# Sliding-window attention and soft MoE in one program: 64 queries x 8 heads in a group, and values on 64x64 tiles

## The chip, the cores and the metric

The kernel runs on one core of a Trainium2 chip. The metric is the time of one execution in microseconds, the median of three runs. The engines are named as the profile names them: PE (TensorE, matmuls; PEld is its weight load), ACT (ScalarE), DVE (VectorE), POOL (GpSimd) and SP (SyncE), from which nearly all DMAs are issued. PE writes to PSUM only; the other engines carry results from there to SBUF.

## The reference: what is computed

There are B=8 batches, H=8 heads, S=576 positions and D=64 features per head; everything is f32.

```
scores = (q @ k.T) / 8 - slope[h] * |i - j|      # only where 0 <= i - j < 128, else -1e9
attn   = softmax(scores);  x = attn @ v          # x: 4608 tokens x 512 features
logits = x @ phi                                 # phi: 512 x 32 slots (8 experts x 4)
d = softmax over tokens (axis 0) of logits;  slot_input = d.T @ x
slot_out[e] = relu(slot_input[e] @ w1[e]) @ w2[e]        # 512 -> 1024 -> 512
c = softmax over slots (axis 1) of logits;   out = c @ slot_out
```

A query sees itself and the 127 positions before it. The weights w1 and w2 are 33.5 MB, q, k, v and the output 9.4 MB each.

## The kernel before

*Tiles and groups.* The tokens are cut into 36 tiles of 128 queries, `(b, t)`. t=0..3 are the four full blocks of a batch; t=4 (in odd batches) holds the 64 last queries of the batch before and of this one. A tile is worked in two groups, g=0 and 1, of 4 heads each: 72 groups of 128 queries x 4 heads. A group's four heads lie in PSUM as `s4[:, u]`, u = 0..3, one bank pair (`s4s`) for even groups and one for odd ones.

*Scores.* `scores` writes for each strip of 32 queries only the 160 keys in its window: bf16 matmuls with `ramp` lay down the distance penalty (L236), then q by k is added (L247), eight small tiles of 64 rows x 32 columns of the array side by side. So in columns 0 to 127 stand the keys of the block before, in 128 to 255 those of the block itself, and each query uses exactly 128 of them. `merge` puts these together in one place with a predicated copy of 4 x 128 columns (`copy_predicated`, L262 for t=1..3, L264 for t=4, L260 for t=0), `rowmax` and `bias` make the negative scaled maximum `nb`, and `expo` takes four exponentials of 128x128 on ACT, each with a row sum (`accum_out`, the ACTIVATION_READ_ACCUMULATOR in the trace).

*Values.* Two groups later `flip` transposes the four 128x128 blocks on PE into bank "pt", `split` copies them to SBUF on ACT and separates them on POOL into the part of the block itself (`pa`) and of the block before (`pp`), zeros elsewhere. Three groups later `values` multiplies both by v (L362; L367 for t=4) into bank "xp": per head and block a 128x128 weight load and 64 moving columns. `x_store` scales by the inverse row sums (`total` on POOL, `inverse` on DVE) and puts x into SBUF, `x_flip` and `x_keep` transpose it for the logits.

*The token work* comes once for four tiles: `logits`, a running maximum over tokens (`token_max`), exponentials, two transposes, `slot_sum` (d.T @ x) and `slot_add`; and the softmax over slots (`slots_max`, `slots_exp`, `slots_norm`) into `ln`.

*The end.* The last tiles drain, the lanes of the running maximum are joined, `slot_inputs` makes the experts' inputs; then come `hidden` (L734), `expert_out` (L770) and `combine` (L791) with the stores, in the order that `TAIL_ORDER` spells out; `turn` transposes parts of `ln` for `combine`.

*What sets the order.* Inside `manual_schedule` each engine runs its instructions in the order in which the code issues them, and SP its DMAs. One iteration of the main loop issues the softmax front of group i, the flip of i-2, the values of i-3 and the scores of i+1; `do(when, i, ...)` hangs the token work onto later iterations. Banks are single: whoever wants to write "pt", "xp", "xq" or "mi" waits until the reader of the last contents is done. The weights come in units of 512 KB: 36 into a ring (`wpool`) during the attention, 15 into SBUF that the attention has freed (`place`), 13 more into ring slots that `hidden` has freed.

Of the kernel before, what the change touches and what calls it, by code (L numbers as in the profile page):

```python
# [24 lines left out]
P = 128  # L25
NT = 5
# [26 lines left out]
TAIL_ORDER = '''s0 b0v b1a b2v e1n e13 k0 e12 c00 e15 c01 e16 s1 c02 e2n e24 k1 e22 c10 e25 c11 e25 s2 c12 e3n e34 k2 e32 c20 e35 c21 e35 s3 c22 k3 c30 c31 c32'''  # L53
# [11 lines left out]
def tile_attn_softmoe(  # L65
# [4 lines left out]
    vd: bass.AP,  # L70
    phid: bass.AP,
    w1d: bass.AP,
    w2d: bass.AP,
    slopes: bass.AP,
# [11 lines left out]
    mask_u = cst[:, 0:P].bitcast(I32)  # L86
    mask_t = cst[:, P:P + TAIL].bitcast(I32)
    delta = cst[:, P + TAIL:]
    pick, sel = cst[:, 0:P], cst[:, P:P + 2 * NS]
# [11 lines left out]
    kq = cpool.tile([P, 3 * UW], F32, name="kq")  # L101
    ramp = cpool.tile([P, 2, 2, WIN], BF16, name="ramp")
    ones = cpool.tile([P, P], BF16, name="ones")
    kt = cpool.tile([P, 6 * P], F32, name="kt")
    area = cpool.tile([P, 24, HW], F32, name="area")
# [3 lines left out]
    qs = [kq[:, NB * P + 2 * P * i:NB * P + 2 * P * i + 2 * P] for i in range(3)]  # L109
# [5 lines left out]
    vs = [area[:, i] for i in (7, 0, 1, 5)]  # L115
    v3_even, v4_even, v4_odd = area[:, 2], area[:, 3], area[:, 4]
    p4s = [quarters(area[:, i]) for i in (8, 9, 6)]
    pps = [quarters(area[:, i]) for i in (10, 11)]
    pas = [quarters(area[:, i]) for i in (12, 13)]
    xns = [area[:, i] for i in range(14, 14 + NXN)]  # L120
    xts = [quarters(area[:, i]) for i in range(20, 24)]
# [3 lines left out]
    areas = {i: area[:, i:i + 2].rearrange("p a w -> p (a w)") for i in range(0, 24, 2)}  # L125
    place = [ks[1], ks[0], ks[2]] + [areas[i] for i in (0, 14, 2, 4, 10, 8, 12, 6, 20, 22, 16, 18)]
# [20 lines left out]
    groups = [(b, t, g) for b, t in tiles for g in range(2)]  # L147
    number = {key: i for i, key in enumerate(groups)}
    n = len(groups)
# [8 lines left out]
    def load_q(i, eng=None):  # L158
        p, o = i // 18, 2 * P * (i % 18)
        (eng or nc.sync).dma_start(qs[i % 3], qd[p, :, o:o + 2 * P])  # L160
# [8 lines left out]
    v_slot = {}  # L169

    def load_v():
        if len(v_taken) < len(v_loads):
            b, t = v_loads[len(v_taken)]
            v_slot[b, t] = vs[len(v_taken) % 4]
            v_taken.append((b, t))
            nc.sync.dma_start(v_slot[b, t], vd[b, P * t:P * t + P])

    def load_v_tails(b):
        nc.sync.dma_start(v3_even, vd[b, 3 * P:4 * P])
        nc.sync.dma_start(v4_even[0:TAIL], vd[b, 4 * P:S])  # L180
        nc.sync.dma_start(v4_odd[0:TAIL], vd[b + 1, 4 * P:S])

    v_taken = []

    with tc.manual_schedule(engines=ORDERED):
        warm = area[:, 8].bitcast(BF16)[:, 0:512]
        nc.vector.memset(warm, 0.0)
        nc.vector.memset(low, LOW)
        nc.vector.memset(ramp, 0.0)
        nc.vector.memset(ones, 1.0)  # L190
        nc.gpsimd.memset(cst[:, 0:P], 1.0)
        nc.gpsimd.affine_select(cst[:, 0:P], cst[:, 0:P], [[1, P]], ALU.is_gt, 0.0, base=0, channel_multiplier=-1)
        load_k(0, 0)
        load_q(0, nc.scalar)
        for par in range(2):
            nc.sync.dma_start(ramp[64 * par:64 * par + 1], slopes[par:par + 1])
        load_q(1, nc.scalar)
        load_q(2, nc.scalar)
# [5 lines left out]
        nc.gpsimd.memset(area[:, 9, 0:P], 1.0)  # L204
# [5 lines left out]
        for t in range(2, 4):  # L210
            load_k(0, t)
# [343 lines left out]
    def loads(i):  # L555
# [3 lines left out]
        if i < 3:  # L559
            load_v()  # L560
# [362 lines left out]
```

## Time and profile before

| | |
|---|---|
| median of 3 runs | 322.65 us (322.46 to 322.69) |
| profiled execution | 324.43 us, its span 322.7 us |
| granted PE clock, mean | 0.96 |
| PE, DVE, ACT, POOL busy | 305.7, 181.8, 187.5, 85.3 us |
| DMA | 74.37 MB, mean 230 GB/s |
| first scores / last scores of the attention end | 5.85 / 245.96 us |
| first hidden-layer matmul | 264.15 us |

A line of the timeline gives start and duration in us, engine, source line, operation, what is written from what, and a count of instructions that were merged into it; in brackets the idle time ahead and who ended it. An f32 matmul shows as two records. A line of the groups has the busy time in us, the mean of one in ns and the idle time before it. A line of the windows gives start:end, its length, then the busy time of PE, PEld, DVE, ACT and POOL (with counts), the granted PE clock, the DMA engines' share and GB/s.

### The profile page before, as it was taken

Reading aid. Unit: us, or ns where it says so; the run is one execution under the profiler, and the core shown is the slowest. Engines: PE = TensorE matmul, PEld = TensorE weight load, DVE = VectorE, ACT = ScalarE, POOL = GpSimd, SP = SyncE. Lnnn points to the kernel's source line nnn. Section 1 sums busy time; section 2 is a strip of 40 time slices with the busy share of each in tenths; the row PEclk is TensorE's granted clock in tenths of the full one; section 3 lists DMA queues with packets and bytes.
Section 4 is the critical chain, followed back from the end, with each engine's and each line's share of the span. In section 5 each row is a group of like instructions: output and inputs, shape, how many; then the busy total and the mean of one; then the engine's idle time right before and its main releaser. Section 6 shows DMA issues by size and latency. Waiting matters only on the chain.

```text
span 322.7 us, 12515 instructions
## 1 busy us (share of the span) xinstructions
PE 305.7 (95%) x5143; PEld 241.8 (75%) x5143; DVE 181.8 (56%) x443; ACT 187.5 (58%) x769; POOL 85.3 (26%) x162
## 2 busy tenths in 40 slices
PE   7799999999999999999999999999999779999983
PEld 4589888988798799788979888888987623266641
DVE  3544666657675675776577567566746331124452
ACT  2746676677766866786767678766767310003342
POOL 2024413350431334234314342433434001000000
PEclk9659999999999999999999999999999975999998
DMA  7663345786686858687676786786524995995888
GB/s 204 219 182 112 105 148 165 219 282 212 206 307 199 264 175 261 201 281 238 204 240 203 235 257 216 232 258 189 174 72 130 359 387 163 331 399 199 333 346 314
DMA packets 35164, 74.37 MB, mean 230 GB/s; under 512 B 4226, under 2 KB 14116, under 8 KB 35108
## 3 DMA queue, kind: packets, MB, share of 16 engines
q1 hardware_dynamic: 34388, 73.07, 67.9%
q8 instruction: 40, 0.66, 0.8%
q10 hardware_dynamic: 720, 0.51, 0.5%
q14 instruction: 16, 0.13, 0.1%
HBM read 64.13 MB, written 9.44 MB: 228 GB/s over the span
## 4 chain that ended last, share of the span: by engine, by line
PE 88%; DVE 6%; issue 2%; ACT 1%; POOL 1%; DVEq 0%; ACTq 0%; POOLq 0%
PE xp L362 29%; PE pt L327 10%; PE s L247 9%; PE xq L382 6%; PE hp L734 6%; PE op L770 5%; PE s L236 4%; PE po L791 4%; PE ap L449 3%; PE lp L392 3%; PE xp L367 2%; PE s L229 2%; DVE area L373 1%; DVE s L282 1%; PE dp L414 1%
## 5 line engine op out<-in xcount | busy, mean ns | idle before, releaser
L317 ACT ACTIVATE area<-s,nb 128x128 f32<-128x128 f32 x288 | 102.5, 375 | 19.9 <-DVE nb L285 12.9
L362 PE MATMUL xp<-area 128*128 128x64 f32 x880 | 107.2, 275 | 0.0
L362 PEld LDWEIGHTS xp<-area 128*128 128x128 f32 x880 | 105.5, 195 | 0.0
L334 ACT COPY area<-pt 128x512 f32<-128x512 f32 x71 | 41.8, 588 | 56.8 <-PE pt L327 55.0
L317 ACT ACTIVATION_READ_ACCUMULATOR area<-s,nb 128x1 f32 x288 | 61.1, 212 | 0.0
L282 DVE TENSOR_REDUCE s<-s 128x4 f32<-128x512 f32 x71 | 49.6, 699 | 2.4
L336 POOL TENSOR_SCALAR_AFFINE_SELECT area<-area 128x512 f32<-128x512 f32 x48 | 30.6, 637 | 76.2 <-ACT area L334 75.9
L262 DVE COPY_PREDICATED s<-cst,s 128x512 f32<-128x512 int32 x48 | 33.2, 692 | 30.2 <-PE s L247 30.2
L327 PE MATMUL pt<-unit_r,area 128*128 128x128 f32 x284 | 46.0, 285 | 0.6 <-issue 0.4
L247 PE MATMUL s<-kq 64*32 64x160 f32 x1664 | 42.4, 306 | 0.0
L327 PEld LDWEIGHTS pt<-unit_r,area 128*128 128x128 f32 x284 | 32.9, 144 | 7.8 <-issue 5.2
L373 DVE TENSOR_TENSOR area<-xp,rs 128x512 f32<-128x512 f32 x35 | 24.1, 689 | 19.4 <-PE xp L362 16.2
L338 POOL TENSOR_SCALAR_AFFINE_SELECT area<-area 128x512 f32<-128x512 f32 x48 | 30.7, 639 | 3.3
L247 PEld LDWEIGHTS s<-kq 64*32 64x32 f32 x1664 | 29.7, 109 | 0.7
L289 POOL TENSOR_SCALAR rs<-sm 128x8 f32<-128x8 f32 x36 | 10.1, 280 | 74.0 <-ACT area L317 59.0
L382 PEld LDWEIGHTS xq<-unit_r,area 128*128 128x128 f32 x140 | 15.2, 143 | 14.2 <-DVE area L373 11.1
L382 PE MATMUL xq<-unit_r,area 128*128 128x128 f32 x140 | 23.1, 288 | 1.8 <-DVE area L373 1.4
L236 PE MATMUL s<-ramp,ones 64*32 64x320 bf16 x448 | 18.9, 314 | 2.0 <-ACT area L317 1.9
L385 ACT COPY area<-xq 128x512 f32<-128x512 f32 x35 | 20.4, 583 | 0.5 <-PE xq L382 0.5
L797 DVE COPY ob<-po 128x384 f32<-128x384 f32 x24 | 12.4, 553 | 12.4 <-PE po L791 12.4
L734 PE MATMUL hp<-w,inp 128*8 128x512 f32 (+1 forms) x128 | 18.6, 690 | 0.4 <-DVE inp L534 0.4
L260 DVE COPY_PREDICATED s<-cst,fine 128x512 f32<-128x512 int32 (+1 forms) x17 | 11.3, 664 | 11.9 <-PE s L229 7.6
(124 smaller groups left out, 288.0 us busy)
## 6 DMA issues: line engine op xcount, KB each, us to landing
w<-w SPq DMA_DIRECT2D x49, 512.0 KB, 5.1
area<-v_n SPq DMA_DIRECT2D x36, 256.0 KB, 3.6
out<-ob SPq DMA_DIRECT2D x24, 384.0 KB, 3.4
kq<-q_t SPq DMA_DIRECT2D x69, 128.0 KB, 3.1
kq<-k_t SPq DMA_DIRECT2D x32, 256.0 KB, 3.8
area<-w SPq DMA_DIRECT2D x12, 512.0 KB, 6.6
kt<-k_t SPq DMA_DIRECT2D x4, 384.0 KB, 3.8
kq<-w SPq DMA_DIRECT2D x3, 512.0 KB, 4.6
```

The costliest lines, as they stand in the source:

```text
L236: nc.tensor.matmul(s4[32 * c:32 * c + 32, 2 * par:2 * par + 2, 32 * r:32 * r + WIN], lhsT=ones[rows, 0:32], rhs=ramp[rows, g], start=True, ...
L247: nc.tensor.matmul(s4[32 * c:32 * c + 32, 2 * par + jj, 32 * r:32 * r + WIN], lhsT=qt[rows, jj, 32 * c:32 * c + 32], rhs=keys, start=False ...
L262: nc.vector.copy_predicated(s4[:, :, P:2 * P], bc(mask_u, 1, 4), s4[:, :, 0:P])
L282: nc.vector.tensor_reduce(st[key]["mx"][:, us], merged(key, us), axis=AX.X, op=ALU.max, negate=True)
L317: nc.scalar.activation(s["p4"][:, u], merged(key, u), AF.Exp, bias=s["nb"][:, u:u + 1], scale=SCALE, accum_out=st["sm", k][:, h:h + 1],)
L327: nc.tensor.transpose(s["pt"][:, u], s["p4"][:, u], ident)
L334: copy(pa[:, us], s["pt"][:, us])
L336: nc.gpsimd.affine_select(pp[:, us], pa[:, us], [[0, m], [-1, P]], ALU.is_gt, 0.0, base=0, channel_multiplier=1)
L338: nc.gpsimd.affine_select(pa[:, us], pa[:, us], [[0, m], [1, P]], ALU.is_ge, 0.0, base=0, channel_multiplier=-1)
L362: nc.tensor.matmul(xp[:, cols], lhsT=src, rhs=v_slot[b, t - 1 + ph][:, cols], start=(ph == 0 or t == 0), stop=(ph == 1))
L382: nc.tensor.transpose(st["xq", k][:, P * j:P * j + P], xns[k % NXN][:, P * j:P * j + P], ident)
L734: nc.tensor.matmul(hp[nb][NS * c:NS * c + w], lhsT=inp[:, o:o + w], rhs=wt[0, 4 * g + c, 2 * nb + kk][:, 512 * kp:512 * kp + 512], start=( ...
```

## The change

*Groups* become 64 queries x 8 heads: group g of a tile holds the strips g and g+2 of 32 queries. PSUM partitions are (head pair j, 32 queries), and `u` is (head parity, strip). The two groups of a tile are issued together, one iteration of the main loop is now a whole tile k: chains of k, flips of k-1, x_flip of k-3, `values` of k-2, scores of k+1, `values_off` of k-1.

*Merge.* Every query strip's window of 160 keys now starts at the same column, so only 32 columns have to be merged (`mask_le`, `mask_gt`), and exponentials read 128 columns from there. `t == 0` needs no other merge: the penalty ramp holds -1e30 where there are no keys.

*Row sums* come from a column of ones in v (66 columns per head, `VD`); exponentials have no `accum_out`, `total` and `inverse` go, and `x_store` adds EPS, takes the reciprocal and multiplies, per parity.

*Values.* Exponentials are written so that after the flip each 64x64 quarter is either full (it lies wholly inside the window) or triangular. `values_off` multiplies the full ones as soon as they are copied; `values` multiplies the triangular ones, once for the block before (`pps`) and once for the block itself, after `split` has cut them on POOL, in halves of 64 partitions and 256 elements. Both use 64x64 tiles of the array, four of them side by side. t=0 has no block before and uses 128x64.

*Banks* are "a", "b", "e", "o": the flips of the two groups go to "a" and "b", x_flip and slot_sum to "a" too, logits and the token flips to "b", the values to "e" and "o" by head parity. `x_keep` moves from ACT to DVE.

*Loads.* q comes in one DMA per tile (256 KB) into two buffers; the ring has 35 units, 15 go to freed places, 14 to freed ring slots; `sel` is loaded at the start. The penalty ramp and the masks come by DMA.

*The end.* `spin` issues bf16 matmuls of zeros between the steps of the drain; two of the three parts of `ln` are turned there already; `TAIL_ORDER` keeps the third.

The diff, cut to its core:

```diff
-TAIL_ORDER = '''s0 b0v b1a b2v e1n e13 k0 e12 ...
+TAIL_ORDER = '''s0 b2v e1n e13 k0 e12 ...
+VD = D + 2
...
+    def scores(k, g):
+        for par, rows in enumerate(half):
+            for j in range(NPAIR):
+                nc.tensor.matmul(
+                    parts[par][32 * j:32 * j + 32, :, 0:WIN], lhsT=slope[rows, j],
+                    rhs=steps[rows, 1 + 2 * g:3 + 2 * g] if t == 0 else bc(steps[rows, 0], 1, 2),
+                    start=True, stop=False)
+        for rr in range(2):
+            for par, rows in enumerate(half):
+                for j in range(NPAIR):
...
+                        r, o = g + 2 * rr, 0
+                        keys = kall[rows, 4 * (t - 1) + r:4 * (t - 1) + r + 5, j]
                     nc.tensor.matmul(
+                        parts[par][32 * j:32 * j + 32, rr, KB * o:WIN], lhsT=qt[rows, j, rr],
+                        rhs=keys, start=False, stop=(rr == 1))
...
+    def merge(k, g, us=ALL):
+        m = len(range(4)[us])
+        dst, src = (P, 0) if g else (0, P)
+        nc.vector.copy_predicated(
+            window(k, g, us, dst, KB), bc((mask_le, mask_gt)[g], 1, m), window(k, g, us, src, KB))
...
+            nc.scalar.activation(
+                dst, window(k, g, u, KB * g, P).rearrange("p (a w) -> p a w", a=2), AF.Exp,
+                bias=s["nb"][:, u:u + 1], scale=SCALE)
...
+    def take(k, g, copy):
+        copy(
+            pas[k % 2][:, :, :, KB * g:KB * g + KB],
+            st[k, g]["pt"].rearrange("p u (j w) -> p u j w", j=NPAIR))
+    def split(k, g):
+        for hf, rows in enumerate(half):
+            pa = pas[k % 2][rows, 2 * hf:2 * hf + 2, :, cols]
+            pp = pps[k % 2][rows, :, :, cols]
+            nc.gpsimd.affine_select(
+                pp, pa, [[0, 2 * NPAIR], [-1, KB]], ALU.is_gt, 0.0, base=-KB * g, channel_multiplier=1)
+            nc.gpsimd.affine_select(
+                pa, pa, [[0, 2 * NPAIR], [1, KB]], ALU.is_ge, 0.0, base=KB * g, channel_multiplier=-1)
...
+    def values_off(k, to=None):
+        for j in range(NPAIR):
+            for hf, par, rr in four(k):
+                nc.tensor.matmul(
+                    st["x", k][par][half[rr], j], lhsT=pas[k % 2][rows, places(k).index(2 * par + rr), j],
+                    rhs=v[rows, par, j], start=(j == 0), stop=False)
+    def values(k, to=None):
+        for j in range(NPAIR):
+            for kind in range(2):
+                for hf, par, rr in four(k):
+                    nc.tensor.matmul(
+                        st["x", k][par][half[rr], j], lhsT=pa[rows, at, j] if kind else pp[rows, at % 2, j],
+                        rhs=v[rows, par, j], start=False, stop=(j == NPAIR - 1 and kind == 1))
+    def x_store(k, pars=(0, 1)):
+        for par in pars:
+            nc.vector.tensor_scalar_add(rs[:, par], xp[par][:, :, D], EPS)
+        nc.vector.reciprocal(rs[:, pars[0]:pars[-1] + 1], rs[:, pars[0]:pars[-1] + 1])
+        for par in pars:
+            nc.vector.tensor_tensor(x[:, par], xp[par][:, :, 0:D], bc(rs[:, par], 2, D), op=ALU.mult)
...
+            chain(k, 1)
+            if k:
+                flip(k - 1, 0, "a")
+                flip(k - 1, 1, "b")
+                run("turn", k)
+            if k:
+                take(k - 1, 0, nc.scalar.copy)
+                split(k - 1, 0)
+                expo(k, 0)
+                take(k - 1, 1, nc.scalar.copy)
+                split(k - 1, 1)
+            run("keep", k)
+            expo(k, 1)
+            if k >= 2:
+                values(k - 2)
+            run("mid", k)
+            if k + 1 < n:
+                scores(k + 1, 0)
+                scores(k + 1, 1)
+                loads(k + 1)
+            if k >= 2:
+                after_values(k - 2)
+                x_store(k - 2)
+            if k:
+                values_off(k - 1)
...
+        spin(1)
+        turn(0, "a", free[1])
```

How the order on the engines moves, at three places. First PE in a steady tile. Before, on the way from one group's scores to the next (`xq` is x_flip, `pt` the flips, `xp` the values, `s_0` and `s_1` the scores' banks):

```order
L382 MATMUL xq<-unit_r,area 128x128 [waits DVE_49]
L382 MATMUL xq<-unit_r,area 128x128 x3
L327 MATMUL pt<-unit_r,area 128x128 [waits PE_49]
L327 MATMUL pt<-unit_r,area 128x128 x3
L362 MATMUL xp<-area 128x64 [waits DMAHW3_49,PE_49]
L362 MATMUL xp<-area 128x64 x3
L236 LDWEIGHTS ones
```

After, from the end of one tile's scores to the start of the next ones (L345 is `values_off`, L368 `values`, L305 the flips, L388 x_flip):

```order
L345 MATMUL xp<-va,area 64x66 [waits DVE_49,PE_49]
L345 MATMUL xp<-va,area 64x66 [waits DVE_49]
L345 MATMUL xp<-va,area 64x66 [waits DMAHW2_49]
L345 MATMUL xp<-va,area 64x66 x13
L305 MATMUL pt<-unit_r,area 128x128 x8
L388 MATMUL xq<-unit_r,xs 128x128 [waits Activation_49]
L388 MATMUL xq<-unit_r,xs 128x128 x3
L368 MATMUL xp<-va,area 64x66 [waits Pool_49] x2
L368 MATMUL xp<-va,area 64x66 x3
L368 MATMUL xp<-va,area 64x66 [waits Pool_49]
L368 MATMUL xp<-va,area 64x66 x26
```

The x_flip stood ahead of a group's flips and waited for DVE's x_store; now it stands behind the flips of both groups and waits for ACT, whose copy empties bank "a". `values_off` waits for DVE, which empties the banks "e" and "o".

Second, PE in a tile with the token flips (L439) and slot_sum (L451), after; before, the token flips (L414, L438) stood in two other groups and had a bank of their own ("mi"):

```order
L305 MATMUL pt<-unit_r,area 128x128 [waits Activation_49]
L305 MATMUL pt<-unit_r,area 128x128 x3
L439 MATMUL dp<-unit_r,lg 128x128 [waits Activation_49]
L439 MATMUL dp<-unit_r,lg 128x128
L388 MATMUL xq<-unit_r,xs 128x128 [waits DVE_49]
L388 MATMUL xq<-unit_r,xs 128x128
L388 MATMUL xq<-unit_r,xs 128x128 [waits DVE_49]
L388 MATMUL xq<-unit_r,xs 128x128
L356 MATMUL xp<-va,area 64x66 [waits DMAHW2_49]
L356 MATMUL xp<-va,area 64x66 x15
L451 MATMUL ap<-xs,dn 32x512 [waits DVE_49,Activation_49]
L451 MATMUL ap<-xs,dn 32x512 x3
```

The token flips now stand between the flips and x_flip, in bank "b", which the second flip has just filled and ACT must copy first; slot_sum waits for bank "a" and for the copied token flips.

Third, DVE. Before, for a tile without token work (L262 or L264 is the merge, L292 the inverse, L373 x_store):

```order
L264 COPY_PREDICATED s_0_84<-cst,s_0_84 128x4x64 [waits DMAHW7_49,PE_49,Activation_49]
L282 TENSOR_REDUCE s_0_84<-s_0_84 128x4 [waits DVE_49]
L285 TENSOR_SCALAR nb<-s_0_84 128x4 [waits DVE_49]
L373 TENSOR_TENSOR area<-xp,rs 128x512 [waits PE_49]
L264 COPY_PREDICATED s_1_85<-cst,s_1_85 128x4x64 [waits PE_49,Activation_49]
L282 TENSOR_REDUCE s_1_85<-s_1_85 128x4 [waits DVE_49]
L285 TENSOR_SCALAR nb<-s_1_85 128x4 [waits DVE_49]
```

After (L264 is the merge of 32 columns, L272 and L276 maximum and bias, L391 x_keep, L379 to L382 x_store):

```order
L264 COPY_PREDICATED s_0_86<-cst,s_0_86 128x4x32 [waits PE_49,Activation_49]
L272 TENSOR_REDUCE s_0_86<-s_0_86 128x4 [waits DVE_49]
L276 TENSOR_SCALAR nb<-s_0_86 128x4 [waits DVE_49]
L264 COPY_PREDICATED s_1_87<-cst,s_1_87 128x4x32 [waits PE_49,Activation_49]
L272 TENSOR_REDUCE s_1_87<-s_1_87 128x4 [waits DVE_49]
L276 TENSOR_SCALAR nb<-s_1_87 128x4 [waits DVE_49]
L391 COPY xs<-xq 128x512 [waits PE_49]
L379 TENSOR_SCALAR rs<-xp 128x4 [waits PE_49]
L379 TENSOR_SCALAR rs<-xp 128x4
L380 RECIPROCAL rs<-rs 128x8 [waits DVE_49]
L382 TENSOR_TENSOR xs<-xp,rs 128x256 [waits DVE_49]
L382 TENSOR_TENSOR xs<-xp,rs 128x256
```

x_keep has joined DVE and stands ahead of x_store, which has grown from one instruction to five; both chains of the tile stand ahead of them.

More of the change, by code (lines that the diff above doesn't have):

```diff
@@ L146, in tile_attn_softmoe @@
     tiles = [(b, t) for b in range(B) for t in order(b)]
-    groups = [(b, t, g) for b, t in tiles for g in range(2)]
-    number = {key: i for i, key in enumerate(groups)}
-    n = len(groups)
+    n = len(tiles)
     v_loads = [(b, t) for b in range(B) for t in range(4)]
@@ L322, in flip, with chain @@
[L322 to L335 removed]
+    def chain(k, g):
+        merge(k, g)
+        rowmax(k, g)
+        bias(k, g)
@@ L653, in tile_attn_softmoe, with spin @@
+            for _ in range(4):
+                filler()
+        ka, kb, kc = n - 3, n - 2, n - 1
+        lp = free[3]
+        idle = inp.bitcast(BF16)[:, 0:512]
+        def spin(m):
+            if "spin" not in st:
+                st["spin"] = bank("o", [P, 512], "spin")
+            for _ in range(m):
+                nc.tensor.matmul(st["spin"], lhsT=idle[:, 0:P], rhs=idle, start=True, stop=True)
         for _ in range(3):
             load_weight()
-        nc.sync.dma_start(pick[0:NS], seld[0:NS, 2 * NS:])
@@ L656, in tile_attn_softmoe @@
-        nc.sync.dma_start(sel, seld[:, 0:2 * NS])
-        x_store(ka)
-        inverse(kb)
+        nc.gpsimd.memset(inp, 0.0)
+        flip(kc, 0, "a")
+        flip(kc, 1, "b")
+        take(kc, 0, nc.scalar.copy)
+        take(kc, 1, nc.vector.tensor_copy)
+        x_flip(ka)
+        x_keep(ka)
+        values(kb)
+        for _ in range(5):
+            load_weight()
+        values(kc, [x.rearrange("p (j d) -> p j d", d=P)[:, :, 0:VD] for x in (free[0], free[2])])
+        x_store(kb)
+        run("act", n)
@@ L659, in tile_attn_softmoe @@
         run("dve", n)
+        x_store(kc, (0,))
+        x_store(kc, (1,))
         drain()
-        nc.gpsimd.memset(inp, 0.0)
-        flip(gc, to=quarters(free[0]))
-        load_weight()
-        split(gc, LO, nc.scalar.copy)
-        split(gc, HI, nc.vector.tensor_copy)
-        x_flip(ka)
-        values(gb, to=free[1])
-        x_keep(ka)
-        values(gc)
-        load_weight()
-        load_weight()
-        logits(final, range(3), to=lp)
-        x_store(kb, slice(0, 4))
-        x_store(kb, slice(4, 8))
@@ L675, in tile_attn_softmoe @@
-        x_flip(kb, free[2], range(0, 2))
-        x_flip(kb, js=range(2, 4))
-        x_keep(kb, nc.scalar.copy, slice(0, 2))
-        x_keep(kb, nc.vector.tensor_copy, slice(2, 4))
+        for _ in range(2):
+            load_weight()
+        spin(1)
+        turn(0, "a", free[1])
+        x_flip(kb, bank("b", [P, DM], "xq"))
+        x_keep(kb)
+        spin(1)
+        x_flip(kc, None, range(0, 2))
+        x_flip(kc, None, range(2, 4))
+        x_keep(kc, nc.scalar.copy, slice(0, 2))
+        x_keep(kc, nc.vector.tensor_copy, slice(2, 4))
```

567 lines of the change are left out of this document (253 added, 314 removed).

## The prediction

> **What bounds the kernel now.** I read the page's first and fourth parts, then the windows, then the timeline of one steady stretch.
>
> ```profile
> PE 305.7 (95%) x5143; PEld 241.8 (75%) x5143; DVE 181.8 (56%) x443; ACT 187.5 (58%) x769; POOL 85.3 (26%) x162
> PE 88%; DVE 6%; issue 2%; ACT 1%; POOL 1%; DVEq 0%; ACTq 0%; POOLq 0%
> 100.00:120.00 20.00, 19.99 (x370) 17.17 (x371) 13.44 (x33) 14.71 (x63) 5.68 (x11) 1.00 0.71 218
> ```
>
> TensorE (PE) carries 88% of the chain and is busy for 19.99 of 20 us in a steady window, with VectorE (DVE) at 13.4 and ScalarE (ACT) at 14.7. What it does there, for one group of 128 queries x 4 heads (two groups are a tile, 36 tiles in all):
>
> ```profile
> 109.23 0.42 PEld L382 LDWEIGHTS xq<-unit_r,area 128*128 128x128 f32 x4 [0.84 <-DVE area L373]
> 109.62 0.47 PEld L327 LDWEIGHTS pt<-unit_r,area 128*128 128x128 f32 x4
> 110.05 1.86 PEld L362 LDWEIGHTS xp<-area 128*128 128x128 f32 x16
> 110.42 0.59 ACT L334 COPY area<-pt 128x512 f32<-128x512 f32 x1 [0.48 <-PE pt L327]
> 111.99 0.33 PE L236 MATMUL s<-ramp,ones 64*32 64x320 bf16 x8
> 112.01 0.53 PEld L247 LDWEIGHTS s<-kq 64*32 64x32 f32 x32
> 112.79 0.42 PEld L327 LDWEIGHTS pt<-unit_r,area 128*128 128x128 f32 x4 [0.25 <-issue]
> ```
>
> From start to start: flips 0.43, values 1.94, scores 0.80, so 3.17 us a group without a hole. The values take most. Their 16 records (an f32 matmul is two records) need 0.116 us each, because each loads 128x128 weights for 64 moving columns. The scores put eight small tiles side by side: 32 records in 0.53, 16.6 ns each.
>
> **The change, part by part.** *Values.* Per tile of kind t=1..4 the 32 (t=4: 64) records become 96 on 64x64 tiles: 64 in `values`, 32 in `values_off`. No row shows 64x64. The nearest:
>
> ```profile
> 242.14 0.54 PEld L229 LDWEIGHTS s<-kq 64*128 64x128 f32 x8
> 247.91 1.01 PEld L367 LDWEIGHTS xp<-area 128*64 128x64 f32 x32 [0.17 <-issue]
> 235.13 0.81 PEld L392 LDWEIGHTS lp<-area,phi 128*32 128x32 f32 x32 [0.25 <-issue]
> 236.14 0.42 PEld L327 LDWEIGHTS pt<-unit_r,area 128*128 128x128 f32 x4 [0.20 <-issue]
> 261.04 1.07 PE L449 MATMUL ap<-area,dn 128*32 128x512 f32 x8
> ```
>
> Two column halves side by side give 31.6 ns a record (L367), two row halves 67 ns against 116 (L229). Both together lie between 31.6 (row halves gain nothing) and 15.8 (they gain fully); L229's 1.7-fold gain puts it at 18, the scores' eight tiles at 16.6. I take 17: `values` 1.09 us, `values_off` 0.54, 1.63 together, where two groups now take 3.88.
>
> L392, four tiles side by side, keeps 0.81/32 = 25.3 ns; there each tile streams 128 columns twice, so it says little of 66.
>
> The Trainium skill ("TensorE: Matmul & The Clock Gate", "Wait — 56ns, not 53.3ns?") says that matmuls never start closer than about 25 ns, however small. The scores' row with 16.6 ns disagrees for tiles side by side; by the rule the values would come to 2.4 us a tile instead of 1.63.
>
> *The other engines.*
>
> ```profile
> L317 ACT ACTIVATE area<-s,nb 128x128 f32<-128x128 f32 x288 | 102.5, 375 | 19.9 <-DVE nb L285 12.9 <-DVE cs L481 3.4 <-DMA phi<-phi 3.4
> 110.90 0.31 ACT L474 ACTIVATE ln<-ln 128x128 f32<-128x128 f32 x1
> 111.11 0.58 ACT L385 COPY area<-xq 128x512 f32<-128x512 f32 x1
> L282 DVE TENSOR_REDUCE s<-s 128x4 f32<-128x512 f32 x71 | 49.6, 699 | 2.4
> L262 DVE COPY_PREDICATED s<-cst,s 128x512 f32<-128x512 int32 x48 | 33.2, 692 | 30.2 <-PE s L247 30.2
> L264 DVE COPY_PREDICATED s<-cst,s 128x256 f32<-128x256 int32 x8 | 3.4, 427 | 6.9 <-PE s L247 5.5 <-ACT area L317 1.3
> L285 DVE TENSOR_SCALAR nb<-s 128x4 f32<-128x4 f32 x71 | 11.4, 161 | 2.9
> L292 DVE RECIPROCAL rs<-rs 128x8 f32<-128x8 f32 x36 | 6.9, 192 | 0.0
> L373 DVE TENSOR_TENSOR area<-xp,rs 128x512 f32<-128x512 f32 x35 | 24.1, 689 | 19.4 <-PE xp L362 16.2
> L373 DVE TENSOR_TENSOR area<-s,rs 128x256 f32<-128x256 f32 x2 | 0.8, 420 | 2.1 <-PE s L362 2.1
> L338 POOL TENSOR_SCALAR_AFFINE_SELECT area<-area 128x512 f32<-128x512 f32 x48 | 30.7, 639 | 3.3
> L205 POOL TENSOR_SCALAR_AFFINE_SELECT unit_r<-area 128x128 fp32r<-128x128 f32 x1 | 0.3, 293 | 0.1
> ```
>
> ACT's exponentials lose the accumulator read: 0.21 apart (L474 to the next start) instead of 0.35, 8 per tile; x_keep leaves ACT. 2x0.49 for the copies + 8x0.21 = 2.7 us. DVE: the merge of 32 columns is 128 elements, 0.30 on the line through L264 and L262 (0.16 to 0.43 if bent). A chain is 0.30+0.70+0.16 and hand-overs, 1.22; two are 2.44; x_keep comes to DVE, 0.69; x_store grows from 0.69 to 1.30 (0.24 for two additions of 4 columns, 0.19, 0.76 for two products, gaps). Together 4.4, and some 0.8 of token work: 5.2. POOL: 8 selects of 256 elements, 0.41 each between 0.29 and 0.64: 3.3. All three run beside PE, if X, the time of a tile, stays above their sums.
>
> *One steady tile*, zero at the first flip of iteration k. PE: 8 flips to 0.85; x_flip uses bank "a", so waits for the first copy: flip to copy start 0.80, copy 0.59, hence 1.44 (a hole of 0.59), to 1.86; 0.1 for the change of tile shape; `values` to 3.05; two score groups (2x0.80 less the drain between them, 0.13 of the 0.25 in the row) from 3.13 to 4.60; `values_off` to 5.14; next flip at 5.25. `values_off` must wait for x_store: `values` 3.05 + 0.25 + 1.30 = 4.60, just in time. DVE's next chains are ready 0.5 and 1.7 after the next flip, ACT wants them at 1.3 and 2.7. The scores want the exponentials at 3.13 and 3.80; they end at 2.3 and 3.7. So X = 5.25 (4.66 without the hole), and PE is still first, now with a wait in it that was not there: x_flip and all the work behind it stand still until ACT's copy is out of bank "a".
>
> Every fourth tile has logits, +1.01 (L392 to the next flip). Another has the token flips, which stand on bank "b" and so wait for the second copy: 0.80+0.49+4x0.21+0.59 = 2.77 instead of 1.44, plus 0.21 for themselves and 1.0 for slot_sum (L449): +2.55. Tiles of t=0 have no `values_off` and narrower scores: -1.05.
>
> *Loads.* q comes a tile at a time, v with 66 columns for 64, one weight unit fewer ahead of the end. Nearly the same bytes in 5.85/6.78 of the time raise the DMA share of the steady window from 0.71 to 0.82: hidden, with holes left. On SP q is asked for as soon as the scores two tiles earlier have freed its buffer, some 10 us ahead of its use, the v tile and the k block behind it; the weights stand last in each iteration. If a q came late, the scores would wait on PE with all that is behind them; I price it at nothing, and at 1 us a tile, +32, if that cover were gone.
>
> *Head and end.*
>
> ```profile
> 8.00:16.00 8.00, 5.87 (x80) 4.50 (x88) 4.59 (x10) 6.15 (x30) 0.20 (x1) 0.63 0.68 223
> 16.00:24.00 8.00, 8.00 (x101) 6.64 (x81) 3.91 (x8) 3.31 (x14) 1.88 (x4) 0.52 0.60 182
> 15.33 0.95 PEld L247 LDWEIGHTS s<-kq 64*32 64x32 f32 x32
> 28.25 0.73 PE L247 MATMUL s<-kq 64*32 64x160 f32 x32
> 245.35 0.61 PE L229 MATMUL s<-kq 64*128 64x128 f32 x8
> 257.87 1.06 PE L392 MATMUL s<-area,phi 128*32 128x128 f32 x8 [0.92 <-DVE area L385]
> 264.15 1.92 PE L734 MATMUL hp<-w,inp 128*32 128x512 f32 x2 [0.35 <-DVE inp L534]
> 262.00:266.00 4.00, 3.02 (x11) 1.12 (x7) 1.16 (x4) 0.00 (x0) 0.00 (x0) 0.58 1.02 366
> 266.00:270.00 4.00, 4.00 (x20) 1.82 (x23) 0.96 (x6) 0.00 (x0) 0.00 (x0) 0.50 0.35 137
> 269.28 0.17 PEld L734 LDWEIGHTS hp<-w,inp 128*8 128x8 f32 x4 [0.68 <-issue]
> 274.08 0.11 PEld L734 LDWEIGHTS hp<-w,inp 128*8 128x8 f32 x4 [0.32 <-issue]
> ```
>
> Tile 3's scores end at 28.98 now, the last (tile 35) at 245.96: 32 tiles, 6.78 each. At the head PE is at half clock (0.63 and 0.52 in the two windows; the scores' weights take 0.95 instead of 0.53). I take the same clock for the new kernel. The first chains, in halves as now, let tile 1's scores end at 10.2. Then, with PE's times doubled: flips of tile 0 to 12.2, its copies and tile 1's exponentials on ACT to 14.5, tile 2's scores to 15.8; flips, ACT and the values of tile 0 to 20.2, tile 3's scores to 23. Bounds: 21 (as if the clock rose one tile earlier) and 27 (four times the 6.8 of a tile now).
>
> From the last scores to the first hidden layer there are 18.2 us now. Afterwards a whole tile drains, from zero at the last scores: `values_off`, flips, token flips, x_flip, `values` to 5.5; slot_sum 6.6; slot_add on DVE, behind x_store, 8.0; only then is bank "a" free for the last flips (8.9) and copies (9.9); `values` of the last two tiles to 12.3; x_store in two halves 14.3; the slot norm, which stands ahead of the last x copy on DVE, 15.3; the copy 15.7; logits of the last lane 16.9; and the chain that now runs from 258.93 (the end of L392) to 264.15, 5.2, with spins among it 5.4: 22.3. Bounds: 18.2, as now, and 26 (one more tile's drain).
>
> From 264.15 to 322.7 there are 58.55. Four hidden records took 0.85 at half clock, 0.43 later. `spin` fills the holes that stand ahead of the drop. If the clock holds: 2.65 for the 5.3 us of hidden behind 267.6, 0.9 for its first records and 0.45 for the slot inputs, 4.0; two transposed parts leave the path, 0.8: 53.75. If not: 57.75. The 24 stores are untouched.
>
> Sum: 23 + 32x5.25 (168.0) + 8x1.01 + 7x2.55 - 6.7 (six t=0 tiles and one's scores) = 210.3; + 22.3 = 232.6; + 53.75 = 286.4 us of span. The profiled run took 324.43 for a span of 322.7; the runs shown have a median of 322.65, the span itself, so the forecast is 286.5.
>
> **Rivals.** *Row halves do not load side by side* at 64 columns: 31.6 ns a record, 96 x 14.6 ns x 28 tiles = +39 us: 326, slower. It decides from 30.4 ns on ((322.65-286.5)/2688 + 17). L229's 67 ns for two halves speaks against it. *A floor between starts*: if 64-column tiles can follow each other only as L392's do, 25.3 ns, 96 x 8.3 ns x 28 = +22: 308.5; against it stands the 16.6 ns of the scores. (The skill's figure above would be this case.) *DVE takes over*: 5.2 us of sum beside X of 5.85 on average, with x_store ahead of `values_off` and of the next chain; holes of 0.45 a tile put it at 301 (297 to 306). The same row L373 speaks for it: the two 256-column products cost 0.84 for 0.69. The Trainium skill ("TensorEngine Tiling (Array Packing)", "PSUM Bottleneck") warns that tiling speeds up the matmuls and not the emptying of PSUM; that is this rival. *The holes are shorter*, as DVE and ACT answer earlier than by my hand-overs: without the copy hole (32 x 0.59) and the token one (7 x 1.33) 258; part of it 260 to 277. *The change does less for the clock*: the gate stays at half longer at the head or drops in the drain: 290 to 297, in the first case's range.
>
> **Numbers.** As forecast, 277 to 297: 0.58. Shorter holes: 0.14. DVE first: 0.13. Floor between starts, 304 to 313: 0.08. Row halves serial, 322 to 330: 0.05. Others, above 306: 0.02. Range 268 to 309: it leaves out half of the shorter holes, a third of the floor, the serial case. What a measurement can tell here from no change is 0.2%, 0.65 us: faster 0.94, same 0.01, slower 0.05.
>
> **What would show it.** The 32 records of `values_off` span 0.5 to 0.6 us, `values` 1.0 to 1.2; x_flip shows a wait of about 0.6 for ACT's copy, the token flips one of 1.3 or more; the last scores lie near 210, the hidden layer near 233, at full clock. I am wrong if values' records stand 25 or 31 ns apart, if `values_off` waits long for DVE's products, if exponentials stand further apart than 0.21, or if PE's clock is half inside the tiles.

## The result: slower, 349.1 us, and the profile after

The changed kernel takes 349.1 us (median of four, 342.2 to 352.8) where the kernel before takes 322.67 (322.5 to 323.4). The ratio, 1.067 with a 95% interval of 1.055 to 1.079, leaves out the two of the four runs that lie over 1.5% above the shortest, and so stands for some 344 us. The forecast was 286.5. The profiled execution is the longest of the four, 352.79 us with a span of 351.1, so the parts of its time that are added up below belong to that one run; the runs lie much further apart than those of before. The page of the changed kernel, its first, third and fourth parts (busy time, the queue of PE's instructions, the chain by engine):

```profile
PE 280.8 (80%) x7422; PEld 203.1 (58%) x7424; DVE 189.3 (54%) x583; ACT 142.1 (40%) x448; POOL 100.7 (29%) x234
q8 instruction: 58, 0.95, 1.1%
PE 68%; issue 12%; ACT 12%; DVE 5%; DMA 2%; ACTq 0%; DVEq 0%
```

PE does less work than before (280.8 us for 305.7) in more instructions: 14,846 matmuls and weight loads for 10,286. And 12% of the chain is "issue": PE stands and waits for nothing that the profile names. The row of q8 is the key. It is the DMA queue on which PE's own program comes in; the same row of the page before reads

```profile
q8 instruction: 40, 0.66, 0.8%
```

58 packets of 16,384 bytes for 14,846 instructions, 40 for 10,286: one packet is some 256 instructions. Now the attention's windows, before and after (start:end, length, busy PE, PEld, DVE, ACT, POOL, clock, DMA share, GB/s):

```profile
24.00:246.00 222.00, 220.38 (x3990) 191.38 (x3993) 143.91 (x342) 156.60 (x668) 78.35 (x141) 1.00 0.65 206
```

```profile
21.00:273.00 252.00, 200.71 (x5957) 156.00 (x5945) 147.96 (x459) 111.47 (x362) 91.85 (x209) 0.88 0.57 184
```

Before, PE is busy 220 of 222 us at full clock. After, it stands for 51 of 252 us, and the clock is at half for a quarter of the time. The DMA engines are used less than before, not more. The timeline of PE across one of the holes:

```profile
96.27 1.09 PE L305 MATMUL pt<-unit_r,area 128*128 128x128 f32 x8
97.65 0.66 PE L388 MATMUL xq<-unit_r,xs 128*128 128x128 f32 x4 [0.29 <-ACT area L311]
98.24 1.16 PE L368 MATMUL xp<-va,area 64*64 64x66 f32 x64
99.33 0.33 PE L231 MATMUL s<-ramp 64*32 64x320 bf16 x8
99.48 0.73 PE L248 MATMUL s<-kq 64*32 64x160 f32 x32
100.46 0.33 PE L231 MATMUL s<-ramp 64*32 64x320 bf16 x8 [0.26 <-ACT area L286]
100.60 0.72 PE L248 MATMUL s<-kq 64*32 64x160 f32 x21
104.31 0.49 PE L248 MATMUL s<-kq 64*32 64x160 f32 x11 [2.99 <-issue]
104.73 0.70 PE L345 MATMUL xp<-va,area 64*64 64x66 f32 x32
105.36 0.88 PE L305 MATMUL pt<-unit_r,area 128*128 128x128 f32 x4
```

PE stops in the middle of a score group: 21 of 32 records done, then 2.99 us of nothing, then the other 11. The profile names no wait there, and all 32 read the same two tiles, q and k. Counted in order of start, with PE's semaphore waits counted too (14,921 records in all), the stop is at PE record 4801 = 18 x 256 + 193. All 17 "issue" holes of over 0.5 us between 21 us and the last scores stand at such a record, 193 more than a multiple of 256. They sum to 31.9 us. (The other seven holes of over 0.5 us are those ahead of the token flips, below.) What the DMA queues did in three stretches of this hole (98.3 to 101.8, 101.8 to 102.9, 102.9 to 104.3 us; packets, MB, share of the engines):

```profile
q1 hardware_dynamic: 491, 1.25, 94.1%
...
q1 hardware_dynamic: 27, 0.09, 19.3%
q8 instruction: 1, 0.02, 5.4%
...
DMA packets 0, 0.00 MB, mean 0 GB/s; under 512 B 0, under 2 KB 0, under 8 KB 0
```

PE passed the boundary before at 98.31. For 3.5 us data filled the queue (1.25 MB: weights, q and v) and no packet of q8 moved; then one did, 101.91 to 102.86; then nothing at all moved for 1.4 us, and PE went on. Every one of the 17 holes ends 1.2 to 1.6 us after its packet landed. So a round has three parts: from crossing boundary n until the packet starts (1.06 us at the median, 1.24 at most, when data moved for under 15% of that time; 2.42, up to 4.11, when the engines were over half busy), the packet (0.88 to 2.0 us), and 1.4 us. Only then is boundary n+1 crossed: nowhere in this attention earlier than 1.2 us after the packet. The rounds that ended in a hole took 3.9 to 6.5 us; at the forecast's 5.25 us for 376 instructions, PE would use up 256 in 3.6 us.

The holes cost twice. Windows around the same place:

```profile
98.00:101.00 3.00, 2.74 (x134) 2.26 (x135) 2.73 (x10) 2.41 (x9) 2.63 (x7) 1.00 1.04 394
101.00:104.00 3.00, 0.32 (x13) 0.00 (x0) 0.82 (x2) 0.00 (x0) 0.56 (x2) 1.00 0.26 102
104.00:107.00 3.00, 2.69 (x52) 2.09 (x51) 1.15 (x3) 0.67 (x2) 0.00 (x0) 0.78 0.33 92
107.00:110.00 3.00, 3.00 (x85) 2.60 (x88) 0.92 (x3) 2.48 (x9) 0.00 (x0) 0.66 0.89 283
```

Behind the hole the clock is at half (the records give it from 105.65 to 109.06): 85 matmuls in 3 us where there were 134. The same happens behind the token flips, which wait for ACT as forecast:

```profile
47.16 1.09 PE L305 MATMUL pt<-unit_r,area 128*128 128x128 f32 x8
50.01 0.44 PE L439 MATMUL dp<-unit_r,lg 128*128 128x128 f32 x2 [1.76 <-ACT area L311]
50.81 1.89 PE L368 MATMUL xp<-va,area 64*64 64x66 f32 x64
```

The 64 values take 1.89 us there and 1.16 above. In all 61.4 us of the attention are at half clock, in this run.

### The profile page after: what moved, and what is told of

The parts are those of the page before. It is cut to its first block, busy times and chain, and to the rows that moved or that the text cites. A ratio compares the mean times of both kernels' runs of the same rounds, so it can differ in the third digit from the quotient of the medians.

```text
span 351.1 us, 16798 instructions
## 1 busy us (share of the span) xinstructions
PE 280.8 (80%) x7422; PEld 203.1 (58%) x7424; DVE 189.3 (54%) x583; ACT 142.1 (40%) x448; POOL 100.7 (29%) x234
## 4 chain that ended last, share of the span: by engine, by line
PE 68%; issue 12%; ACT 12%; DVE 5%; DMA 2%; ACTq 0%; DVEq 0%
PE s L248 11%; PE xp L368 10%; PE pt L305 8%; PE xq L388 7%; ACT area L311 6%; ACT area L286 5%; PE xp L345 5%; PE op L792 5%; PE s L231 4%; PE hp L756 4%; PE po L813 3%; PE ap L451 3%; PE xp L356 3%; PE lp L398 2%; DMA kq<-k_t 2%
## 5 line engine op out<-in xcount | busy, mean ns | idle before, releaser
L322 POOL TENSOR_SCALAR_AFFINE_SELECT area<-area 64x256 f32<-64x256 f32 x112 | 49.3, 440 | 172.7 <-ACT area L311 168.1
L248 PE MATMUL s<-kq 64*32 64x160 f32 (+4 forms) x2176 | 55.2, 294 | 13.5 <-issue 12.1
L391 DVE COPY xs<-xq 128x512 f32<-128x512 f32 (+1 forms) x34 | 23.2, 682 | 62.0 <-PE xq L388 61.5
L272 DVE TENSOR_REDUCE s<-s 128x4 f32<-128x512 f32 (+1 forms) x73 | 50.5, 692 | 2.5
L324 POOL TENSOR_SCALAR_AFFINE_SELECT area<-area 64x256 f32<-64x256 f32 x112 | 49.4, 441 | 7.7
L305 PE MATMUL pt<-unit_r,area 128*128 128x128 f32 x288 | 45.8, 309 | 2.0 <-issue 1.9
L305 PEld LDWEIGHTS pt<-unit_r,area 128*128 128x128 f32 x288 | 35.7, 156 | 6.7 <-issue 3.9
L368 PE MATMUL xp<-va,area 64*64 64x66 f32 x1792 | 39.3, 246 | 0.3 <-issue 0.3
L368 PEld LDWEIGHTS xp<-va,area 64*64 64x64 f32 x1792 | 34.9, 157 | 6.3 <-issue 4.3
L345 PE MATMUL xp<-va,area 64*64 64x66 f32 x896 | 23.3, 232 | 15.0 <-issue 14.8
L388 PE MATMUL xq<-unit_r,xs 128*128 128x128 f32 x144 | 28.2, 327 | 6.4 <-ACT area L311 5.9
L231 PE MATMUL s<-ramp 64*32 64x320 bf16 x576 | 26.9, 316 | 7.8 <-issue 4.2
L264 DVE COPY_PREDICATED s<-cst,s 128x128 f32<-128x128 int32 (+1 forms) x73 | 21.0, 288 | 21.7 <-PE s L248 21.6
L345 PEld LDWEIGHTS xp<-va,area 64*64 64x64 f32 x896 | 18.0, 139 | 23.8 <-issue 22.6
L382 DVE TENSOR_TENSOR xs<-xp,rs 128x256 f32<-128x256 f32 x70 | 26.4, 418 | 1.2
L388 PEld LDWEIGHTS xq<-unit_r,xs 128*128 128x128 f32 x144 | 19.3, 165 | 13.0 <-ACT area L311 12.3
L379 DVE TENSOR_SCALAR rs<-xp 128x4 f32<-128x4 f32 x70 | 8.1, 156 | 25.3 <-PE xp L368 19.8
```

Of the source, the lines that this page charges most:

```text
L231: nc.tensor.matmul(parts[par][32 * j:32 * j + 32, :, 0:WIN], lhsT=slope[rows, j], rhs=steps[rows, 1 + 2 * g:3 + 2 * g] if t == 0 else bc(s ...
L248: nc.tensor.matmul(parts[par][32 * j:32 * j + 32, rr, KB * o:WIN], lhsT=qt[rows, j, rr], rhs=keys, start=False, stop=(rr == 1))
L272: nc.vector.tensor_reduce(mx, window(k, g, us, KB * g, P), axis=AX.X, op=ALU.max, negate=True)
L305: nc.tensor.transpose(s["pt"][:, places(k).index(u)], s["p4"][:, u], ident)
L322: nc.gpsimd.affine_select(pp, pa, [[0, 2 * NPAIR], [-1, KB]], ALU.is_gt, 0.0, base=-KB * g, channel_multiplier=1)
L324: nc.gpsimd.affine_select(pa, pa, [[0, 2 * NPAIR], [1, KB]], ALU.is_ge, 0.0, base=KB * g, channel_multiplier=-1)
```

## Experiments

Theory: PE starves for instructions, and half clock follows from its holes. Rivals: data come late; the small tiles or the token hole bring half clock by themselves; the holes at record 193 are chance. One table for all runs. The ratios are against the kernel before, run beside each. The columns from "last sc." on come from one traced run a row, which is the longest of its four for the changed kernel and the shortest of its runs for e2, e3, e5 and e10; so a difference between rows counts where the ratios show it too, or where it is well above the 10 us by which the runs of the changed kernel differ. "Last scores" is the start of the last score matmul; holes are those of over 0.5 us at a 256th record between 21 us and there; the delay is the median from a boundary to its packet where the engines were over half busy, and the longest. Where no ratio stands, there was one run, or the whole time says nothing.

```
                       PE instr.  us     ratio (95%)          last sc. holes, us   half clock  delay, max
before                 10286     322.7   1                     245.7    0           2.7        1.06  3.20
after                  14846     349.1   1.067 (1.055-1.079)   273.3   17  31.9    61.4        2.42  4.11
e1  weights late       14846      -                            242.5    9  10.8    27.3        1.37  3.87
e2  bias in one        13984     332.4   1.026 (1.018-1.034)   249.6   11  15.7    27.3        2.42  4.07
e3  weights spread     14846     344.7   1.068 (1.060-1.076)   261.7   15  25.5    37.5        2.02  4.54
e4  e2 + e3            13984     331.4   1.023 (1.016-1.031)   252.7    9  15.0    20.5        1.75  4.62
e5  token flips late   14846     333.9   1.041 (1.029-1.053)   251.3   17  32.4    23.9        2.16  4.85
e6  before, more       13870     340.9   one run               262.1    3   2.9     2.1        1.81  3.46
e7  e2 + e5            13984     317.3   0.988 (0.980-0.997)   238.3   12  17.2    13.7        2.13  4.69
e8  e2 + e3 + e5       13984     315.0   0.974 (0.963-0.985)   238.8    9  13.3    13.7        2.03  3.93
e9  e8, last sum early 13984     311.3   0.967 (0.960-0.974)   232.7   10  10.8     3.4        1.65  3.50
e10 e9, v early        13984     306.7   0.944 (0.936-0.953)   222.9    3   3.2     3.4        1.35  4.07
e11 after, more        19456     407.0   one run               327.3   31  57.5    95.6        2.03  4.27
e12 e1 + e2 + e5       13984      -                            221.3    2   4.2     6.8        1.51  3.65
```

**e1: an emptier queue.**

```diff
-            load_weights_at(k)
...
-        for _ in range(3):
+        for _ in range(NW + 4):
             load_weight()
```

> The changed kernel with the 35 weight loads of the attention issued only behind its last tile, so the attention runs with q, k and v on the queue alone; its whole time says nothing (the experts then wait for the weights), only the attention is read: the start of its last scores, 273.6 us in the changed kernel. Theory (PE starves for instructions: each 256 instructions a 16 KB block must come, and its packet stands behind the data packets): the packet starts within 1.5 us of the block boundary nearly always, the 19 gaps of over 0.5 us at boundaries shrink to a few, PE stays at full clock for most of the attention, last scores at 215 to 235. Rival (q, k or v come late): no less bytes of those are moved, but the queue is emptier, the gaps end with q, k, v landing and last scores come at 235 to 260. Rival (the 64x64 tiles or the token hole alone make PE drop to half clock): the last scores stay within 265 to 275, the clock at 0.8 to 0.9.

```profile
21.00:242.00 221.00, 188.20 (x5959) 145.33 (x5949) 147.80 (x462) 111.93 (x362) 92.87 (x210) 0.94 0.45 142
```

The attention ends 31 us earlier with the same PE program; holes fall from 31.9 to 10.8 us and half clock from 61 to 27. Tiles alone are not what stops PE. The last scores miss the forecast by 7 us and lie in the range that I had given to the rival of late data. Its sign did not come: all nine holes stand at a 256th record and end 1.3 to 1.5 us behind an instruction packet, and at the line of the scores two waits are for data,

```profile
its engine sat idle before it (us, times) until:
  issue: 8.8, 10
  DMA kq<-k_t: 3.0, 2
```

What is left: the bursts of q, k and v still hold a packet up to 3.87 us, and the token tiles take 8.0 to 9.6 us, more than I had counted.

**e2: fewer instructions.**

```diff
-            for j in range(NPAIR):
...
-                    parts[par][32 * j:32 * j + 32, :, 0:WIN], lhsT=slope[rows, j],
...
+                parts[par][:, :, 0:WIN], lhsT=ramp[rows, 0:NPAIR * KB],
...
```

> The changed kernel with the four bias matmuls of each row half (64x32 tiles) written as one 64x128 matmul: 4 records a tile for 16, so 24 PE instructions less of about 376, the same bytes and the same sums. Theory (instruction supply): the attention is paid by blocks of 256 instructions, 6 per cent fewer of them, and less half clock behind fewer gaps: 335 us (326 to 341). Rival (tile forms or clock alone): only the records' own time goes, 12 x 16 ns x 36 = 7 us at most, 342 to 349.

332.4, as the theory had it: 24 instructions fewer a tile bring 17 us by the medians and 13 by the ratios. And that though PE's own work grew. Two score groups take 1.57 us in the changed kernel (43.78 to 45.35, the bias of a group first),

```profile
43.78 0.33 PE L231 MATMUL s<-ramp 64*32 64x320 bf16 x8
44.47 0.32 PE L231 MATMUL s<-ramp 64*32 64x320 bf16 x8
45.35 0.56 PE L345 MATMUL xp<-va,area 64*64 64x66 f32 x18
```

and 1.89 with this edit (62.82 to 64.71 in the rows of e12 below): 0.32 us more a tile, some 11 us, outweighed by holes and clock. That the 64x128 matmul does not run beside the small tiles is how I read this; no run shows it by itself.

**e3 and e4: the weights spread.**

```diff
+                next_half()                      # nc.scalar.dma_start of 256 KB
                 take(k - 1, 0, nc.scalar.copy)
                 split(k - 1, 0)
                 expo(k, 0)
+                next_half()
                 take(k - 1, 1, nc.scalar.copy)
...
             expo(k, 1)
+            next_half()
...
-            load_weights_at(k)
```

> The changed kernel with each 512 KB weight load of the attention cut in two and issued from ACT's program at three places of the iteration (ahead of the first copy, ahead of the second, behind the last exponentials) in place of one burst on SP behind q, k and v. Same bytes, same instructions on PE. Theory (the fetch stands behind queued data): the queue is shorter when a boundary is crossed, packets start within 1 to 2.5 us in place of up to 4.1, last scores 235 to 255, 315 to 332 in all. Rival (data late): q, k and v come no later; 342 to 350. Rival (tile forms, clock): no change, 342 to 352.

> Both edits together: 24 PE instructions fewer a tile and the weights in halves from ACT's program. Theory (instruction supply): 300 to 320, last scores 220 to 240, nearly no gap at block boundaries over 1 us. Rivals: 335 to 345.

Both miss. e3's ratio is that of the unspread kernel, e4's that of e2. The delay falls only from 2.42 to 2.02 us and its longest not at all: v, q and k, 776 KB, are still issued together, and I take that to be why; e10 takes it up.

**e5: the token flips behind the values.**

```diff
-        do("turn", k + 4, token_flips, q)
-        do("keep", k + 4, token_keep, q)
-        do("mid", k + 4, slot_sum, q)
-        do("dve", k + 4, slot_add, q)
+        do("mid", k + 4, token_flips, q)
+        do("act", k + 4, token_keep, q)
+        do("mid", k + 5, slot_sum, q)
+        do("dve", k + 5, slot_add, q)
...
```

In e5, e7 and e8 the last of these sums reads two tiles after weights have taken their place, so part of the output is other; the amount of work is the same.

> The changed kernel with one step of the order moved: the two token flips stand behind the values of their iteration (bank b is free there) in place of ahead of them, their copy behind the exponentials on ACT, slot_sum and slot_add one iteration later. Same instructions, same bytes. In the run with late weights the undisturbed tile took 5.23 us, a tile with token flips 8.8 to 9.6, and half clock came 1 to 3 us behind most of the eight holes of 1.4 to 1.8 us. Theory (instruction supply first, holes of any cause then cost half clock): the eight holes go, 13 us, and the half clock behind them, 8 to 12 us; the gaps at block boundaries stay near 30 us or grow a little as blocks are used up faster: 318 to 332. Rival (half clock is made by the token holes and the gaps at boundaries come from it): the gaps go as well, 290 to 305. Rival (holes are hidden behind the wait for instructions): 340 to 352.

The token holes are gone (no other hole of over 0.5 us is left), half clock falls from 61 to 24 us, and 349.1 becomes 333.9 (by the ratios 8 us less), 2 us above the forecast's range. The holes at boundaries stay, 32.4 us: they do not come from the token hole or the half clock. Two causes, then, that share one consequence.

**e6 and e11: more instructions with hardly any work**, in the kernel before and in the changed one.

```diff
+            for _ in range(4):                   # e6, ahead of the bias, t = 0 left out; e11 in all tiles
+                for par, rows in enumerate(half):
+                    for c, r in enumerate(strips):
+                        nc.tensor.matmul(s4[32 * c:32 * c + 32, 2 * par:2 * par + 1, 32 * r:32 * r + 2],
+                            lhsT=ones[rows, 0:32], rhs=ramp[rows, g, 0:1, 0:2], start=True, stop=True)
```

> The kernel before with instructions added and little work: ahead of the bias matmuls of each score group stand 32 more of them, of two columns, each overwritten by the one that counts; 64 PE instructions a group (weight load and matmul), 128 a tile, about 380 a tile as in the changed kernel, with the 128x128 tiles of the values, the bursts of weights and the order of before. Theory (instruction supply): gaps of over 0.5 us appear at block boundaries, where the kernel before has none, 5 to 20 of them, with half clock behind some. The added records themselves cost some 17 ns each, 32 a group: 30 us; so 358 to 385. Rival (64x64 tiles, the copy hole or the token hole are what stops PE): no gap at a block boundary, full clock from 24 us on, 340 to 355.

> The changed kernel with 32 matmuls of two columns more ahead of the bias of each score group, each overwritten by the one that counts: 128 PE instructions more a tile, as in the kernel before with the same addition, where a record cost 7 ns, 16 us in all with gaps. Theory (instruction supply): every 256 instructions past the rate of the supply cost a whole round, 4 to 5 us, half a round a tile: 36 x 0.5 x 4.5 = 80 us, less what is free now: 390 to 430. Rival (gaps at block boundaries are something else that comes with the data): the records' own time, 13 to 20 us: 355 to 370.

e6, timeline of PE:

```profile
81.41 0.28 PE L237 MATMUL s<-ramp,ones 64*32 64x2 bf16 x32
81.75 0.29 PE L253 MATMUL s<-kq 64*32 64x160 f32 x1
83.32 0.78 PE L253 MATMUL s<-kq 64*32 64x160 f32 x31 [1.27 <-issue]
```

The kernel before, which has no 64x64 tile and no hole at a boundary, gets them, with nothing but more instructions: here at record 3521 = 13 x 256 + 193. But there are three of over 0.5 us, fewer than forecast, with no half clock behind them, and the added records cost some 7 ns each. So the time, 340.9, lies in the range of the rival, and it is the place of the holes alone that speaks against it. A block of 256 still lasts 5.4 us on average there (11,292 instructions in 238 us), above most rounds. In e11 the rate was already at the limit, and the same addition costs 58 us, with 31 holes of 57.5 us and 96 us at half clock: 407.0, inside the theory's 390 to 430 and far from the rival's 355 to 370.

**e7 to e10: together.** e7 is e2 and e5; e8 adds e3; e9 is e8 with the last sum ahead of those weights; e10 moves one line of e9:

```diff
                 values(k - 2)
+                after_values(k - 2)              # the load of the next v
             run("mid", k)
...
-                after_values(k - 2)
                 x_store(k - 2)
```

> Bias as one 64x128 matmul (24 PE instructions fewer a tile) and the token flips behind the values. Theory: the two savings add up nearly (16 to 20 us of the first as measured, 15 to 25 of the second): 303 to 316. Rival (holes hidden behind the wait for instructions): 325 to 333.

> As the run before it, with the weight loads in halves from ACT's program. The spread alone was worth 0 to 5 us, less than the theory had it, since packets still started up to 4.5 us behind the boundary. Theory: 300 to 316, within 4 us of the run before it.

> Bias as one 64x128 matmul, token flips behind the values, weights in halves from ACT's program; the sum of the last four lanes stands behind the values of the last tile but one, ahead of the expert weights that take those tiles' place. Theory: as the run with the same three edits, 310 to 317, below the kernel before by 1 to 4 per cent.

> As the run before it, with the load of the next v block ahead of q and k on SP (it waits for the values alone, 1.5 us earlier than q's wait for the scores), so that the burst of v, q and k is cut in two. Theory (a fetch stands behind what is queued): shorter delays in busy stretches, 1 to 2 us at the median for 2.0, 2 to 8 us less than the run before it. Rival (the delay is not set by what is queued): the same time within 1 us.

```profile
21.00:223.00 202.00, 185.21 (x5608) 133.40 (x5607) 150.12 (x464) 111.39 (x365) 93.30 (x212) 0.99 0.73 231
```

e7 ends 1 us above its range and far from the rival's; e8 and e9 lie in theirs. e10 has the PE program, the bytes and the tiles of e9; only v is asked for ahead of q, by 2.1 us at the median, where e9 has it 0.9 us behind. The median delay goes from 1.65 to 1.35 us, the holes from 10.8 to 3.2, the time from 311.3 to 306.7, and the intervals of the two ratios do not meet. (The traced run of e10 is its shortest, 301.4 us, so the fall of the holes is in part that of one run; the longest delay did not fall.) The rival's 1 us is out: what is queued when matters by itself. With the three edits of e9 the kernel is 5.6% faster than before (0.944, 0.936 to 0.953).

**e12: everything away.**

> The changed kernel with late weights, one bias matmul for four and the token flips behind the values: fewest instructions, emptiest queue, no token hole; the attention alone is read. If instruction supply, the token hole and half clock behind both are all that the forecast missed, the last scores come where it had them less what the token hole was priced there (7 x 1.33 = 9) : 202 to 216, and PE keeps full clock nearly throughout. If the steady tile was wrong as well, they stay above 225.

A full tile of e12, from first flip to first flip:

```profile
59.75 1.09 PE L304 MATMUL pt<-unit_r,area 128*128 128x128 f32 x8
61.14 0.66 PE L387 MATMUL xq<-unit_r,xs 128*128 128x128 f32 x4 [0.29 <-ACT area L310]
61.72 1.16 PE L367 MATMUL xp<-va,area 64*64 64x66 f32 x64
62.82 0.31 PE L230 MATMUL s<-ramp 64*128 64x320 bf16 x2
64.71 0.70 PE L344 MATMUL xp<-va,area 64*64 64x66 f32 x32
65.34 0.33 PE L304 MATMUL pt<-unit_r,area 128*128 128x128 f32 x1
```

One run, with the last sum as in e9. Last scores at 221.3, between the two readings that I had set (216 and 225). 4.2 us are two holes at boundaries, some 3 the half clock behind one of them. The tile is 5.59, not 5.25, nearly all of it by the merged bias: 1.89 us for two score groups, where the forecast had 1.47 and the changed kernel 1.57. Over 32 tiles that is up to 13 us. Together this is the 20 us above the 201 that the forecast gives without token holes (210.3 - 9.3).

## Why the prediction was wrong, point by point

**The failed step: PE was costed by the durations of its records, and nothing for bringing them in.** The sum took a tile from 6.78 to 5.85 us and gave no line to the rise from some 245 instructions a tile (7983 in 222 us) to 376. The "Loads" paragraph asked whether transfers would be late for PE's operands and priced them at nothing; that was right for q, k and v (2% of the chain waits for DMA, nearly all of it two loads of k in the first 8.5 us), and wrong for the transfer that it did not list, PE's own program. The page and the trace before had most of what was needed: 40 packets on q8 for 10,286 instructions, 7.1 us a block on average in the attention, with packets already starting up to 3.2 us behind their boundary. At 5.25 us for 376 instructions a block would last 3.6 us. A packet that starts 3.2 us late and takes 0.9 is past that before it has landed. The rest of the round, 1.4 us, shows only in traces with holes. None of the rivals named this; the slower one, row halves that load one after another, did not happen.

The Trainium skill ("Runtime: NRT & Kernel Launch", "Instruction fetch mechanics") says that the sequencer brings the program in by blocks of 16 KiB, 256 instructions, over a DMA queue of its own while it executes the present block, and that crossing a boundary is mostly hidden, because dispatch is slower than the fill. The trace agrees on the block and the queue. It does not agree on the rest here: 31.9 us stand open, since the small tiles side by side went at 17 ns for a load and a matmul (64 of each in 1.09 us).

**The second: what a hole costs.** The token flips start 2.85 us behind the first flip (47.16 to 50.01), where I had 2.77; the hole is 1.4 to 1.8 us for 1.33. But I priced a hole at its own length. Half clock also followed it, so such a tile took 9.5 us (47.16 to 56.70) for 7.80. Half clock inside the tiles stood among the signs of being wrong, but the prediction had a price for the clock only outside the tiles. The sum for the last scores was 210.3; 273.3 were measured, in the longest run. 31.9 of the 63 are holes at boundaries, up to 30.7 the 61.4 us at half clock (less where holes lie inside), 2.5 the token holes, 3 the scores, less 2 at the head; these overlap by some 3.

**Right:** `values` 64 records in 1.09 us (98.24 to 99.33; 1.09 forecast), `values_off` 0.63 for 0.54 (104.73 to 105.36); so row and column halves do load side by side, and neither the serial case nor the floor of 25.3 ns came. x_flip starts 1.38 us behind the first flip (96.27 to 97.65) for 1.44, the score groups take 1.57 for 1.47. DVE did not take over (5% of the chain). One small miss cost little: exponentials start 0.25 us apart at the median, not 0.21. The end, by the first hidden-layer piece of the chain and the last scores' line:

```profile
L248 PE MATMUL s<-kq x2176: 188/296/473, 5.0 to 273.3; 64*32 64x160 f32 x151, 64*32 64x32 f32 x12, 64*32 64x96 f32 x12, 64*32 64x128 f32 x12
297.59 10.51 PE hp L756 x96
```

From 273.3 to 297.59 are 24.3 us for 22.3, and from there to the span's end at 351.1 are 53.5 for 53.75. The clock is full from 266.1 to 344.6, as was hoped of the spins (no run leaves them out), and 5 us of the gain that was forecast arrived. The head is 2 us better than forecast, at full clock where half was assumed; why is open.

## What to carry to other kernels

Before replacing large matmuls by many small ones, take the time that PE will need for 256 of its instructions, matmuls and weight loads counted, and hold it against the round of an instruction packet that the trace shows (boundary to packet, packet, packet to resume; 3.9 to 6.5 us in the changed kernel, where a hole ended it). If it is shorter, count instructions as a cost, merge what can be merged, and take loads out of bursts: one of three was worth 4.6 us here (e10), while halving the weights alone brought nothing that the ratios show (e3). An "issue" hole in the middle of matmuls with the same inputs, at every 256th record of PE, is the sign.

## What the runs showed of the hardware that I had not expected

An instruction packet in effect stands behind data that are already queued: with idle DMA engines it starts about 1.1 us behind the boundary, in a burst up to 4.85. PE goes on 1.2 to 1.6 us after it lands (57 of 57 holes in the traces of the changed kernel, e1 and e11).

About half a stretch of idle PE was enough to lose half the clock. On the 3.41 us grid of the clock records, in seven traces (after, e1, e2, e5, e9, e10, e11), counting the stretches at full clock from 21 us to the first hidden-layer matmul, every one of 30 with 1.85 us or more of idle PE was followed by half clock, and 23 of 41 with 1.38 to 1.85 us; below that two, both in the drain. The Trainium skill ("TensorE: Matmul & The Clock Gate", "What's actually happening") gives a free-running window of 3413 ns, and the grid agrees; it has the drop come after an idle window, and here half-idle ones did it.
